# Swapping two DMA queues, a second weight set one part earlier, and another pacing of staged rows in a fused long-convolution and mixture-of-experts kernel

## Chip, cores and metric

The kernel runs on one core of a Trainium2 chip. The metric is the time of one execution in device microseconds (us); lower is better. Engines are named as in the profile: PE (matrix engine; PEld its weight loads), DVE (vector), ACT (scalar), POOL (GpSimd) and SP (which here only issues DMAs). A "q" behind an engine's name, as in ACTq, means its instruction queue.

## What is computed

```python
def _attn_ref(x, h):                      # x: (8, 5696, 128), h: (5696, 128), float32
    L = 2 * S
    Yf = np.fft.rfft(x, n=L, axis=1) * np.fft.rfft(h, n=L, axis=0)[None]
    return np.fft.irfft(Yf, n=L, axis=1)[:, :S, :]

def _moe_ref(x, w_gate, w1, w2):          # x: (45568, 128), 8 experts, hidden width 1024
    logits = x @ w_gate
    expert_idx = np.argmax(logits, axis=1)
    ...                                   # probs = softmax(logits), gate_w = probs of the chosen expert
    for e in range(E):
        mask = expert_idx == e
        out[mask] = gate_w[mask, None] * (np.maximum(x[mask] @ w1[e], 0.0) @ w2[e])
    return out
```

The output of the convolution is the token list of the second part: 8 x 5696 = 45568 tokens, each of which goes through one of 8 experts.

## The kernel before

The 8 batches are worked in three groups of 2, 3 and 3 (g0, g1, g2). A group goes through three stages. Stage a (`steps_a`) transforms 48 slices of a batch and stores them to DRAM (`U`). Stage b (`phase_b`) goes over 120 frequency items: it loads `uq` from `U`, makes `xp` on PE, multiplies by the filter on DVE, adds on POOL (`combine`; for the first `ALONE` = 20 items of g2 on DVE), transforms back (`vp`), copies on ACT (`save`, tile `vt`) and stores to `V`. Stage c (`phase_c`) makes token rows from `V`, finds each row's expert, and scatters the rows with indirect DMAs from POOL into `SR`, where rows are sorted by expert; `sort_one` issues one such scatter, and the rows still to be scattered stand in the list `sorts`. Stage a of the next group runs inside stage c of this one (`Guest`). In the text a1 is stage a of g1, b2 stage b of g2, and so on.

Beside this run the experts (`pipeline`): tiles of 256 sorted rows. One tile is loaded (`load`, tile `xr`, 7 buffers), transposed (`turn`, PE tile `mx`), and goes through four steps, each with six matmuls of `layer1` and six of `layer2`; in between, `relu` on ACT and DVE makes `hs`. `drain` copies the result on ACT (`ot`), `turn` transposes it back, `emit` scales it into `xr`, and two indirect DMAs from POOL (`deliver`) scatter the 256 rows to `out`. The four weight pieces of an expert (512 KB each) are loaded by `load_w`, under a condition that skips the load where the expert stays the same.

Tiles become available in parts: a part closes when a given slice of a group is sorted (`HALVES`), and `tables` then works out on DVE, in row vectors of one partition, which rows and which expert each of its tiles has. With the constants of before the parts have 37, 39, 28 and 81 tiles (182 of the 185 run always). The first three have one set of weight buffers, loaded from ACT's queue; the last has two, used in turn, loaded from SP's queue (`sets`, `home`).

While a stage c runs, POOL is taken by the sort, so finished expert tiles are not scattered but stored to DRAM (`leave`, array `STG`); the flag `state["defer"]` says so. Afterwards `recall` loads them back (tile `xb`), one every `BACK` = 6 steps of the pipeline, and their scatters join the same list `pending` as the fresh ones.

The order of instructions on each engine's queue is fixed when the program is made: `run` interleaves the streams by planned costs in units of `STEP`. One expert step costs one `STEP`, one item of stage b `MIX_B[g]`, one step of stage c `MIX_C[g]` (half of that after the last slice), and `HEAD` and `LEAD` are pauses of 8 and 6 steps at the start of stages b and c of g1 and g2. `SETTLE` is the planned pause of 8000 ns between the last sort scatter of a part and its first load. These costs set only the order; in the chip each engine takes its queue in order and waits for what it needs.

Of the kernel before, what the change touches and what calls it, by code (L numbers as in the profile page):

```python
# [29 lines left out]
RW = 130  # L30
# [40 lines left out]
def conv_moe(ctx: ExitStack, tc: tile.TileContext, I, out, B, S, D, E, F, split):  # L71
# [146 lines left out]

    rest_of = [nc.vector]
# [39 lines left out]
    def steps_a(gr, tag, bufs):  # L259
# [28 lines left out]
        def flush():  # L288
            while late:
                nc.sync.dma_start(*late.pop(0))  # L290
# [10 lines left out]
        def store(m):  # L301
# [7 lines left out]
            cp(uts[c][:, :, b * D : (b + 1) * D], srcv)  # L309
# [106 lines left out]
    def phase_b(gr):  # L416
# [3 lines left out]
        def load_m(qb):  # L420
# [6 lines left out]
            else:  # L427
                mt = sb.tile([K2, QB, P], F32, tag="mt", name=f"mt{g}_{q}", bufs=MT)
# [20 lines left out]
        state, banks, late = {}, {}, []  # L449
# [53 lines left out]
        def product(n):  # L503
# [17 lines left out]
            state[n] = (zt, xs)  # L521

        def combine(n):
            zt, xs = state[n]
            eng = nc.vector if g > 1 and n < ALONE else nc.gpsimd
            eng.tensor_tensor(out=zt, in0=zt, in1=xs, op=ALU.add)  # L526

        def inverse(n):
# [3 lines left out]
            zt, _ = state.pop(n)  # L532
# [4 lines left out]
        def save(n):  # L537
# [4 lines left out]
            nc.scalar.copy(outs_[qb][:, k0, c * cw : (c + 1) * cw], banks.pop(n)[:K2, :cw])  # L542
# [21 lines left out]
        for n in range(N + BLAGS[3] + 2):  # L564
# [12 lines left out]
            while late:  # L577
                nc.sync.dma_start(*late.pop(0))
# [17 lines left out]
    state["alone"], state["prepped"], state["defer"], state["now"] = True, False, False, 0  # L596
# [43 lines left out]
    def phase_c(gr, guest=None, after=None):  # L640
# [8 lines left out]
        state["defer"] = g > 0  # L649
# [64 lines left out]
        def turned(n, k):  # L714
# [3 lines left out]
            nc.scalar.copy(yts[n][:, k * cb : (k + 1) * cb, :], tv)  # L718
# [123 lines left out]
        for n in range(n_end + 1):  # L842
            for k in range(nsub):
# [56 lines left out]
        state["alone"] = state["defer"] = False  # L900

    def tables(pt, base):
# [56 lines left out]
        back = 2 if last else 1  # L959
# [40 lines left out]
    def sets(t):  # L1000
        return 2 if seq[t][0] is parts[-1] else 1
# [20 lines left out]
    def load_w(t, n):  # L1022
        pt, j = seq[t]
        z, fixed = home(t), j < sets(t)
        eng = nc.sync if pt is parts[-1] else nc.scalar
        if n == 0:
            ew = eng.value_load(pt.tab[0:1, 1, j : j + 1], min_val=0, max_val=(E - 1) * P)  # L1027
            ch = None if fixed else eng.value_load(pt.tab[0:1, 2, j : j + 1], min_val=0, max_val=1)  # L1028
# [7 lines left out]
        eng.dma_start(dst, WD[n, ds(ew, P), :], **kw)  # L1036
# [31 lines left out]
    def relu(t, k):  # L1068
# [7 lines left out]
        hss[t, k] = hs  # L1076

# [20 lines left out]
    leaving, staged, coming = [], [], []  # L1098
    slot = [0]

    def emit(t, count):
# [7 lines left out]
        else:  # L1109
            pending.extend([(xr, 0), (xr, 1)])  # L1110
# [230 lines left out]
```

## Time and profile before

| | us |
|---|---|
| median of 3 runs (2384.26 to 2411.04) | 2392.96 |
| the profiled execution's own time | 2398.87 |
| its span, first to last instruction | 2397.1 |
| PE / DVE / POOL / ACT busy | 2142.3 / 1583.0 / 1205.5 / 1096.4 |
| mean granted TensorE clock, share of full speed | 0.958 |

A busy time is the sum of the stretches in which an engine had an instruction running; a matmul that waits in the array counts as busy. The stages are read off by which lines run when: c0 with a1 to about 470 us, b1 to 770, c1 with a2 to 1050, b2 from 1094 to 1432, c2 to 1720; after that only experts run.

### The profile page before, as it was taken

Reading aid. Unit: us, or ns where it says so; the run is one execution under the profiler, and the core shown is the slowest. Engines: PE = TensorE matmul, PEld = TensorE weight load, DVE = VectorE, ACT = ScalarE, POOL = GpSimd, SP = SyncE. Lnnn points to the kernel's source line nnn. Section 1 sums busy time; section 2 is a strip of 40 time slices with the busy share of each in tenths; the row PEclk is TensorE's granted clock in tenths of the full one; section 3 lists DMA queues with packets and bytes.
Section 4 is the critical chain, followed back from the end, with each engine's and each line's share of the span. In section 5 each row is a group of like instructions: output and inputs, shape, how many; then the busy total and the mean of one; then the engine's idle time right before and its main releaser. Section 6 shows DMA issues by size and latency. Waiting matters only on the chain. (4 is left out here: it accounts for less than half of the span.)

```text
span 2397.1 us, 46980 instructions
## 1 busy us (share of the span) xinstructions
PE 2142.3 (89%) x14070; PEld 1765.9 (74%) x14070; DVE 1583.0 (66%) x3937; ACT 1096.4 (46%) x2389; POOL 1205.5 (50%) x1289
## 2 busy tenths in 40 slices
PE   7799688679999999978999999988788899999997
PEld 4666454346667787766677778887678889999997
DVE  3499645578988677867988875666644444555554
ACT  4577444323333566543334445555333344444443
POOL 5366437755545076672566651766634444333332
PEclk8899999889999999989999999999889999999999
DMA  9999999698987988867899886656344344333330
GB/s 268 285 298 309 272 293 265 187 262 230 241 234 216 248 234 236 256 165 202 221 245 242 236 224 161 168 153 179 95 145 126 121 135 138 112 115 114 111 114 29
DMA packets 245468, 472.46 MB, mean 197 GB/s; under 512 B 34385, under 2 KB 156295, under 8 KB 245216
## 3 DMA queue, kind: packets, MB, share of 16 engines
q1 hardware_dynamic: 207456, 372.03, 55.8%
q10 hardware_dynamic: 13824, 50.34, 6.8%
q0 software_dynamic: 23936, 47.09, 6.6%
q8 instruction: 114, 1.87, 0.3%
q14 instruction: 138, 1.13, 0.2%
HBM read 595.97 MB, written 171.92 MB: 320 GB/s over the span
## 5 line engine op out<-in xcount | busy, mean ns | idle before, releaser
L1073 DVE SCALAR_TENSOR_TENSOR hs<-mh,hs 128x512 fp32r<-128x512 f32 x728 | 502.0, 690 | 455.1 <-ACT hs L1071 371.0
L1065 PE MATMUL mh<-xtb,wb 128*128 128x256 f32 x4368 | 717.8, 300 | 64.0 <-DVE hs L1073 23.8
L1065 PEld LDWEIGHTS mh<-xtb,wb 128*128 128x128 f32 x4368 | 600.5, 193 | 142.5 <-issue 51.4
L1085 PE MATMUL ma<-hs,wb 128*128 128x256 f32 x4368 | 664.7, 289 | 7.8 <-DMA wb<-WD 6.8
L1071 ACT ACTIVATE hs<-mh 128x512 fp32r<-128x512 f32 x728 | 435.7, 599 | 511.0 <-PE mh L1065 348.3
L1085 PEld LDWEIGHTS ma<-hs,wb 128*128 128x128 f32 x4368 | 582.1, 193 | 10.3 <-DMA wb<-WD 8.1
L610 POOL DMA_INDIRECT SR<-rt,pi x384 | 407.7, 1062 | 311.4 <-issue 135.7
L1129 POOL DMA_INDIRECT out<-xr x276 | 270.2, 979 | 554.6 <-DVE xr L1103 500.8
L526 POOL TENSOR_TENSOR zt<-zt,xs 128x384 f32<-128x384 f32 (+1 forms) x340 | 308.5, 912 | 179.5 <-DVE xs L518 112.2
L542 ACT COPY vt<-vp 96x384 f32<-96x384 f32 (+1 forms) x360 | 158.6, 440 | 426.1 <-PE vp L534 331.8
L486 PE MATMUL xp<-uq,mt 96*128 96x384 f32 (+1 forms) x720 | 273.0, 461 | 33.6 <-DMA uq<-U 14.5
L534 PE MATMUL vp<-zt,mi 128*96 128x384 f32 (+1 forms) x720 | 273.9, 462 | 8.2 <-DVE xs L518 2.3
L511 DVE TENSOR_TENSOR zt<-xp,hh 128x384 f32<-128x384 f32 (+1 forms) x360 | 183.4, 509 | 69.3 <-PE xp L486 45.7
L534 PEld LDWEIGHTS vp<-zt,mi 128*96 128x96 f32 x720 | 106.7, 163 | 125.8 <-issue 78.2
L297 PE MATMUL pa<-xc,fcr 120*120 120x512 f32 x576 | 172.4, 432 | 22.4 <-ACT ut L309 10.4
L518 DVE SCALAR_TENSOR_TENSOR xs<-xp,hh 64x384 f32<-64x384 f32 (+1 forms) x360 | 185.5, 515 | 6.8
L516 DVE TENSOR_TENSOR xs<-xp,hh 64x384 f32<-64x384 f32 (+1 forms) x360 | 182.3, 507 | 6.9
L486 PEld LDWEIGHTS xp<-uq,mt 96*128 96x128 f32 x720 | 117.9, 195 | 62.6 <-issue 32.9
L297 PEld LDWEIGHTS pa<-xc,fcr 120*120 120x120 f32 x576 | 102.2, 193 | 60.8 <-ACT ut L309 10.8
L675 DVE TENSOR_TENSOR vr<-vq,vr 120x768 fp32r<-120x768 f32 x96 | 91.8, 958 | 68.9 <-ACT vr L674 46.1
L309 DVE COPY ut<-pa 120x512 f32<-120x512 f32 x96 | 65.6, 686 | 91.9 <-PE pa L297 60.5
L687 PE MATMUL yp<-vr,gcr 120*120 120x384 f32 x576 | 118.1, 340 | 5.7 <-ACT vr L674 2.5
(123 smaller groups left out, 2212.8 us busy)
## 6 DMA issues: line engine op xcount, KB each, us to landing
wb<-WD ACTq DMA_DIRECT2D x416, 512.0 KB
wb<-WD SPq DMA_DIRECT2D x312, 512.0 KB
vq<-V SPq DMA_DIRECT2D x64, 720.0 KB
U<-ut SPq DMA_DIRECT2D x48, 720.0 KB
uq<-U SPq DMA_DIRECT2D x60, 576.0 KB
V<-vt SPq DMA_DIRECT2D x60, 576.0 KB
xr<-SR SPq DMA_DIRECT2D x182, 130.0 KB
xt<-x SPq DMA_DIRECT2D x96, 240.0 KB
```

What stands on the lines that cost most here:

```text
L297: nc.tensor.matmul(banks[m][:QN, :], lhs, rhs, start=(k == 0), stop=(k == len(ops) - 1))
L486: nc.tensor.matmul(xp[:, :cw], mt[:, k0, :], uc, start=True, stop=True)
L511: nc.vector.tensor_tensor(out=zt, in0=x3, in1=hv[:, 0].broadcast_to([P, cb, D]), op=ALU.mult)
L518: nc.vector.scalar_tensor_tensor(out=xs[to], in0=x3[at], scalar=-1.0, in1=him, op0=ALU.mult, op1=ALU.mult)
L526: eng.tensor_tensor(out=zt, in0=zt, in1=xs, op=ALU.add)
L534: nc.tensor.matmul(vp[:K2, :cw], mi[:, k0, :], zt.rearrange("p b d -> p (b d)"), start=True, stop=True)
L610: s = nc.gpsimd.indirect_dma_start(out=SR[:, :], out_offset=IndirectOffsetOnAxis(ap=pi[:, b : b + 1], axis=0), in_=rt[:, b, :], in_offset= ...
L1065: nc.tensor.matmul(hp[:, u, :], wb[:, a, f, :], xt[:, b, :], start=(n == 0), stop=(n == 2))
L1071: done = nc.scalar.activation(hs[:, 0], hp, AF.Relu)
L1073: nc.vector.scalar_tensor_tensor(out=hs[:, 1], in0=hp, scalar=0.0, in1=hs[:, 0].bitcast(F32), op0=ALU.max, op1=ALU.subtract)
L1085: nc.tensor.matmul(accs[t], wb[:, a, f, :], hs[:, b, u, :], start=(k == 0 and u == 0 and n == 0), stop=(k == NPAIR - 1 and u == 1 and n == 2),
L1129: sc = nc.gpsimd.indirect_dma_start(out=out[:, :], out_offset=IndirectOffsetOnAxis(ap=xr[:, s, D + 1 : D + 2].bitcast(I32), axis=0), in_=x ...
```

## The change

- `HALVES`: the second part closes at slice 12 of 24 in place of 14, so that parts have 37, 33, 34 and 81 tiles.
- `PAIRED`: the third part has two weight sets as well. The second set takes buffers of the tag `mt` in place of `ld`, once stage a of g2 is done (`state["spare"]`); the `mt` tiles of b2 take buffers of `xt`, and `xb` tiles take two of `us`.
- All weight loads go to SP's queue. The stores to `U`, `V`, the filter array `HS` and `STG` go to ACT's queue.
- What is left of `sorts` after a stage c is no longer scattered ahead of the next stage b, but one scatter after each `save` of it. In stage c of g0 there is one more `sort_one` a step, and the two extra ones after the last slice are gone. `tables` is finished and `defer` cleared before the next stage b.
- A returned tile waits 4 steps after its load, the next is recalled only when both scatters of the last are out, and returned scatters have a list of their own: one goes out when no fresh one has for two steps, then none for three.
- Planner's costs: b1 0.6 to 0.55, c2 1.8 to 2.2 (`MIX_A` 0.6 to 0.45 is used only if slices of a1 are left over after c0).

```diff
-HALVES = ((16,), (14, 24), (24,))
+HALVES = ((16,), (12, 24), (24,))
-MIX_A = (0.0, 0.6, 0.8)
-MIX_B = (0.0, 0.6, 0.85)
-MIX_C = (1.0, 1.2, 1.8)
+MIX_A = (0.0, 0.45, 0.8)
+MIX_B = (0.0, 0.55, 0.85)
+MIX_C = (1.0, 1.2, 2.2)
-BACK = 6
+PAIRED = 2
...
         def flush():
             while late:
-                nc.sync.dma_start(*late.pop(0))
+                nc.scalar.dma_start(*late.pop(0))
...
-                mt = sb.tile([K2, QB, P], F32, tag="mt", name=f"mt{g}_{q}", bufs=MT)
+                mt = sb.tile([K2, QB, P], F32, tag="xt" if g > 1 else "mt", name=f"mt{g}_{q}", bufs=5 if g > 1 else MT)
...
-            nc.scalar.copy(outs_[qb][:, k0, c * cw : (c + 1) * cw], banks.pop(n)[:K2, :cw])
+            done = nc.scalar.copy(outs_[qb][:, k0, c * cw : (c + 1) * cw], banks.pop(n)[:K2, :cw])
+            if state["late"]:
+                sort_one(done.ins)
...
             while late:
-                nc.sync.dma_start(*late.pop(0))
+                nc.scalar.dma_start(*late.pop(0))
...
-            nc.scalar.copy(yts[n][:, k * cb : (k + 1) * cb, :], tv)
+            done = nc.scalar.copy(yts[n][:, k * cb : (k + 1) * cb, :], tv)
+            if g == 0:
+                sort_one(done.ins)
...
-                if n >= nu:
-                    sort_one()
-                    sort_one()
...
         if guest:
             yield from guest.rest()
+            state["spare"] = g > 0
+        chore(99)
+        state["alone"] = state["defer"] = False
+        state["late"] = True
         if after:
-            yield next(after)
+            yield from after
         while sorts:
...
-        chore(99)
-        state["alone"] = state["defer"] = False
...
     def sets(t):
-        return 2 if seq[t][0] is parts[-1] else 1
+        return 2 if seq[t][0].s >= PAIRED else 1
...
-        eng = nc.sync if pt is parts[-1] else nc.scalar
-            tag, bufs = ("ld", LD) if z else ("wb", 4)
+            tag, bufs = ("mt", MT) if z else ("wb", 4)
-        eng.dma_start(dst, WD[n, ds(ew, P), :], **kw)
+        nc.sync.dma_start(dst, WD[n, ds(ew, P), :], **kw)
...
             _, dst, xr = leaving.pop(0)
-            nc.sync.dma_start(dst, xr)
+            nc.scalar.dma_start(dst, xr)
...
     def recall(count):
-        if coming and coming[0][0] <= count - BACK // 2:
+        if coming and coming[0][0] <= count - 4:
             xr = coming.pop(0)[1]
-            pending.extend([(xr, 0), (xr, 1)])
-        if staged and not coming and not state["defer"] and count % BACK == 0:
-            xr = sb.tile([P, 2, RW], F32, tag="xt", name=f"xb{count}", bufs=5)
+            returned.extend([(xr, 0), (xr, 1)])
+        if staged and not coming and not returned and not state["defer"]:
+            xr = sb.tile([P, 2, RW], F32, tag="us", name=f"xb{count}", bufs=2)
...
-    def deliver():
-        xr, s = pending.pop(0)
+    def deliver(after=None):
+        paced[0] += 1
+        if pending:
+            xr, s = pending.pop(0)
+            if s:
+                paced[0] = 0
+            after = None
+        elif returned and paced[0] > 1:
+            xr, s = returned.pop(0)
+            paced[0] = -1
+        else:
+            return
...
+        if after is not None:
+            tc.add_manual_dep(sc, after.name, SYNC, reason="scatters are spread over the stage")
...
             while nw[0] < min(t + 3, hi) and seq[nw[0]][0].tabled and state["prepped"]:
                 was, n = user[nw[0]], nw[1]
+                if home(nw[0]) and not state["spare"]:
+                    break
```

## Rows read from the trace of the kernel before

**Rows 1.** The page's parts 1 and 2: busy time of each engine, then tenths in 40 slices of 60 us for PE and for the DMA engines.

```profile
PE 2142.3 (89%) x14070; PEld 1765.9 (74%) x14070; DVE 1583.0 (66%) x3937; ACT 1096.4 (46%) x2389; POOL 1205.5 (50%) x1289
...
PE   7799688679999999978999999988788899999997
...
DMA  9999999698987988867899886656344344333330
```

**Rows 2.** Windows by stage, all lines: stretch and length, then busy us (instructions) of PE, PEld, DVE, ACT and POOL, granted clock, share of the DMA engines, GB/s.

```profile
483.00:515.00 32.00, 21.58 (x51) 10.17 (x51) 21.63 (x39) 4.55 (x10) 17.22 (x19) 0.78 1.02 270
515.00:770.00 255.00, 245.43 (x1249) 169.55 (x1248) 226.16 (x415) 92.74 (x202) 134.96 (x135) 0.99 0.89 236
770.00:1050.00 280.00, 261.57 (x1891) 221.88 (x1890) 204.00 (x691) 168.71 (x386) 154.01 (x165) 0.98 0.81 227
1050.00:1094.00 44.00, 27.67 (x171) 25.90 (x170) 21.22 (x95) 10.45 (x24) 27.88 (x34) 0.73 0.71 186
1094.00:1432.00 338.00, 325.47 (x1875) 247.51 (x1874) 295.06 (x546) 133.30 (x281) 188.27 (x188) 1.00 0.88 232
1432.00:1720.00 288.00, 260.23 (x2072) 231.81 (x2071) 179.77 (x662) 152.92 (x360) 161.36 (x176) 0.98 0.60 157
1720.00:1746.00 26.00, 13.72 (x64) 12.84 (x64) 13.77 (x48) 4.33 (x9) 14.65 (x18) 0.57 0.27 74
```

**Rows 3.** Windows of `layer1` alone (L1065; a tile has 24 such matmuls): stretch and length, PE busy (instructions), PEld busy (instructions), clock, DMA share, GB/s.

```profile
0.00:1720.00 1720.00, 368.40 (x2080) 292.90 (x2081) 0.96 0.83 230
...
1746.00:1880.00 134.00, 66.40 (x406) 57.15 (x407) 0.95 0.44 136
1880.00:2040.00 160.00, 82.22 (x542) 71.94 (x541) 0.99 0.42 131
2040.00:2286.00 246.00, 139.63 (x952) 124.55 (x951) 1.00 0.36 116
```

**Rows 4.** PE in the stretch 1746 to 1880 us: its waits for weight loads (us in total, times, longest), then the timeline behind one change of expert (start, length, what; in brackets the idle time ahead of it).

```profile
PE mh L1065 <- DMA wb<-WD: 12.8, 5, 3.6
...
1788.04 1.62 PE L1065 MATMUL mh<-xtb,wb 128*128 128x256 f32 x6 [2.87 <-DMA wb<-WD]
1789.45 1.48 PE L1085 MATMUL ma<-hs,wb 128*128 128x256 f32 x6
```

**Rows 5.** Timelines of POOL, then of PE, between 1954 and 1962 us: scatters of a fresh tile (`xr`) and of a returned one (`xb`), and the transposes `mx` that come once in each tile.

```profile
1957.10 0.97 POOL L1129 DMA_INDIRECT out<-xr  x1 [3.92 <-DVE xr L1103]
...
1959.66 0.97 POOL L1129 DMA_INDIRECT out<-xb  x1 [0.31 <-issue]
1960.94 0.97 POOL L1129 DMA_INDIRECT out<-xb  x1 [0.30 <-issue]
...
1954.64 0.38 PE L182 MATMUL mx<-ident,ot 128*128 128x128 f32 x2
...
1961.77 0.44 PE L182 MATMUL mx<-ident,ot 128*128 128x128 f32 x2 [0.79 <-ACT ot L1095]
```

**Rows 6.** The scatters of returned tiles and their loads, by tile (count; length in ns min/median/max; first and last start).

```profile
L1129 POOL DMA_INDIRECT out<-xb x88: 972/974/1250, 1112.0 to 2043.3; - x88
L1124 SPq DMA_DIRECT2D xb<-STG x44: 203/416/1343, 1090.4 to 2034.5; - x44
```

**Rows 7.** From timelines of SP and POOL, one load of a returned tile and the scatter that waited for it, and the last scatter of the kernel; from SP's waits, its wait at the end (us in total, times, longest).

```profile
2004.61 0.33 SPq L1124 DMA_DIRECT2D xb<-STG  x1
...
2009.85 0.97 POOL L1129 DMA_INDIRECT out<-xb  x1 [2.02 <-DMA xb<-STG]
...
2386.09 0.97 POOL L1129 DMA_INDIRECT out<-xr  x1 [0.30 <-issue]
...
SPq L1337 <- DMA out<-xr: 10.3, 2, 9.4
```

**Rows 8.** Timelines of PE, then of ACT, between c1 and b2.

```profile
1073.93 1.72 PE L1065 MATMUL mh<-xtb,wb 128*128 128x256 f32 x6 [7.38 <-DVE hs L1073]
...
1082.32 1.65 PE L1065 MATMUL mh<-xtb,wb 128*128 128x256 f32 x6 [3.81 <-DVE hs L1073]
...
1073.31 5.06 ACTq L1036 DMA_DIRECT2D wb<-WD  x2
1080.94 0.60 ACT L1071 ACTIVATE hs<-mh 128x512 fp32r<-128x512 f32 x1 [7.35 <-DMA xr<-SR]
```

**Rows 9.** ACT's waits between 480 and 1740 us that ended with a weight load (us in total, times, longest); then, by source line, the DMA instructions of the moved weight loads and `V` stores on the queue that they leave (ns min/median/max).

```profile
ACT vt L542 <- DMA wb<-WD: 40.5, 24, 3.9
...
ACT vr L674 <- DMA wb<-WD: 14.1, 13, 1.9
...
L1036 ACTq DMA_DIRECT2D wb<-WD x416: 88/90/2097, 479.9 to 1870.7; - x139
...
L578 SPq DMA_DIRECT2D V<-vt x90: 305/359/1364, 127.5 to 1429.9; - x90
```

**Rows 10.** The start of b1: timelines of PE, then of POOL.

```profile
483.02 4.62 PE L486 MATMUL xp<-uq,mt 96*128 96x384 f32 x8 [14.10 <-issue]
495.97 1.62 PE L486 MATMUL xp<-uq,mt 96*128 96x384 f32 x2 [8.33 <-DMA uq<-U]
...
488.13 1.00 POOL L610 DMA_INDIRECT SR<-rt,pi  x1 [0.30 <-issue]
489.51 3.91 POOL L526 TENSOR_TENSOR zt<-zt,xs 128x384 f32<-128x384 f32 x4
```

More of the change, by code (lines that the diff above doesn't have):

```diff
@@ L448, in phase_b @@
         cutting = F3[g]
-        state, banks, late = {}, {}, []
+        zts, banks, late = {}, {}, []
         def filt(qb, k0):
@@ L595, in conv_moe @@
     state["base"] = base0
-    state["alone"], state["prepped"], state["defer"], state["now"] = True, False, False, 0
+    state |= {"alone": True, "prepped": False, "defer": False, "late": False, "spare": False, "now": 0}
     sorts, row = [], [0]
@@ L648, in phase_c @@
         vqs, rts, yts, gates = {}, {}, {}, {}
-        state["defer"] = g > 0
+        state["defer"], state["late"] = g > 0, False
         nu = NB // NI
@@ L958, in tables @@
         nc.vector.memset(tab[:, 2, :], 1)
-        back = 2 if last else 1
+        back = 2 if g >= PAIRED else 1
         nc.vector.tensor_tensor(out=tab[:, 2, back:], in0=ej[:, back:], in1=ej[:, : NT - back], op=ALU.not_equal)
@@ L1076, in relu @@
         hss[t, k] = hs
+        return done.ins
     def layer2(t, k):
@@ L1097, in conv_moe @@
     STG = dram.tile([STAGED, P, 2, RW], F32, name="STG")
-    leaving, staged, coming = [], [], []
-    slot = [0]
+    leaving, staged, coming, returned = [], [], [], []
+    slot, paced = [0], [0]
     def emit(t, count):
@@ L1109, in emit @@
         else:
[L1110 removed]
+            pending.append((xr, 0))
+            pending.append((xr, 1))
     def leave(count):
@@ L1172, in pipeline @@
                 recall(len(hist))
-                if pending:
-                    deliver()
-                elif t >= hi and not (any(hist[-1 - LAG :]) or leaving or staged or coming):
+                deliver()
+                if t >= hi and not (any(hist[-1 - LAG :]) or pending or leaving or staged or coming or returned):
                     return
-                yield STEP if turned < nrow or any(hist[-1 - LAG :]) else None
+                busy = pending or leaving or staged or coming or returned or turned < nrow or any(hist[-1 - LAG :])
+                yield STEP if busy else None
                 continue
@@ L1189, in pipeline @@
             yield STEP
+            done = None
             if act:
-                relu(t, k)
+                done = relu(t, k)
                 step = (t, k + 1) if k < NPAIR - 1 else (t + 1, 0)
@@ L1201, in pipeline @@
                 emit(to, len(hist))
-            if pending:
-                deliver()
+            deliver(done)
     def experts():
@@ L1213, in rest @@
     def rest():
-        work = None
         for gr in groups:
-            if work:
-                yield from work
-            guest, work = None, None
-            if gr.g + 1 < len(groups):
-                guest, work = Guest(groups[gr.g + 1]), phase_b(groups[gr.g + 1])
-            yield from phase_c(gr, guest, work)
+            more = gr.g + 1 < len(groups)
+            guest, after = (Guest(groups[gr.g + 1]), phase_b(groups[gr.g + 1])) if more else (None, None)
+            yield from phase_c(gr, guest, after)
     DONE = object()
```

15 lines of the change are left out of this document (8 added, 7 removed).

## The prediction

> **What bounds the kernel now.** I read the page's totals and slices first. PE is busy 89% of the span, no other engine over 66% [rows 1], so a gain must come from stretches where PE idles or runs slowly. The slices show three dips behind the dense start: about 480, 1050 and 1720 us, each where a stage c ends. The DMA engines are nearly full up to 1430 us and about a third busy at the end.
>
> The windows by stage put numbers on it [rows 2]. In b1 and b2 PE is busy 245 of 255 and 325 of 338 us. c1 leaves 18 us idle, c2 28. The two transitions hold more for their length: of 44 us before b2 PE is busy 28, at clock 0.73, and of 26 us after c2 14, at clock 0.57, near the lower level, 1.2 GHz.
>
> The windows of layer 1 give the experts' price [rows 3]. From 2040 us on a tile takes 246 / (952/24) = 6.2 us, with no idle time: the floor. Before it, 1746 to 1880 takes 7.9 us a tile and 1880 to 2040 takes 7.1. Those 294 us hold 39.5 tiles, 245 us of floor work, so 49 us are lost there, the largest block that this change touches. By 1720 us 2080/24 = 86.7 tiles are done, and 95 of the 182 remain.
>
> **The second weight set.** With one set, a new expert's pieces can be loaded only as the old ones fall free. PE waits 12.8 us for this in 1746 to 1880, and behind such a wait groups of six matmuls last 1.48 us, the pace of the lower clock [rows 4], where later ones last 0.88. Some four such groups behind each of four waits cost about 8 us more. The last part already has two sets, but its first loads also wait, some 3 us. The parts before it keep 104 tiles together, so about 17 two-set tiles are left behind c2. I take -22 us (bounds: -24, and 0 if the loads come late anyway). The price is eight more experts' loads of 2 MB in the third part, 16 MB: hidden in c2, whose DMA share is 0.60, and the tail at 0.44 [rows 2, 3]; were that room gone, they would cost 16 MB at 157 GB/s, about 100 us.
>
> **Returned scatters, paced.** The other half of the 49 us: where two fresh and two returned scatters follow one another on POOL, the next transposes come 0.79 us late and 7.1 us after the last, not 6.2 [rows 5]. 26 pairs at about 1 us make 26. The trace doesn't say why, nor show single ones. Two fresh scatters in a tile cost nothing after 2040 us, so a lone one may be free: -26 us. If each costs half a pair, 64 of them in the tail cost 32, or +6 us net. The nearest row is the free one; I take -16.
>
> **The same pacing leaves tiles over.** This I count in the planner's steps. Before, deferral lasts 6 + 48 x 1.2 + 5 x 0.6 + 8 = 75 steps in c1 and 6 + 48 x 1.8 + 5 x 0.9 = 97 in c2; at four steps a tile this makes 43 staged tiles, and the trace has 44 [rows 6]. One comes back every 6 steps: 18 in b2's 108, and 26 in 156 steps behind c2, which is 39 tiles, and so the last returned scatter is at 2043 us [rows 6]. The count holds.
>
> After, c1 defers 67 steps and c2 6 + 48 x 2.2 + 5 x 1.1 = 117: 46 staged. In a tile, fresh scatters take two steps, one step passes, one returned scatter goes. Its second half goes a tile later; the next load is recalled one step after that, needs four, and so just misses the next slot. That makes 12 steps, three tiles, for one staged tile. b2's 116 steps bring back 10, c2 starts with 7 over and ends with 36. The 95 tiles behind it are 380 steps: 32 come back, and about four are left after the last expert.
>
> There PE has nothing to cover them. A load takes 2004.61 to 2009.85, 5.2 us; two scatters 2 x (0.97 + 0.30) = 2.5; and the last scatter lands 9.4 us after it is made [rows 7]. With two buffers a buffer turns in about 17 us. Counted from the last fresh scatter (end 2387, landing at +9), the tile in progress lands at +11, the next at +13; the buffers then give +29, +31 and +46. So three left over cost 22 us, four 36, two 19, one 4. I take +30; bounds 0 (the count is wrong, or they slip in between) and +39.
>
> **Weights off ACT, stores onto it.** ACT waits for weight loads 40.5 us ahead of `vt` and 14.1 ahead of `vr` [rows 9], and in one place this reaches PE: ACT's two loads take 5.06 us, `relu` starts 7.35 late, and PE idles 3.81 [rows 8]. The 7.38 us wait beside it ends with DVE; the tables that keep DVE there stay. Of the 44 us before b2, 171 matmuls are worth 20 at the tail's pace (8.4 per us), so 24 are lost; I take -8 (bounds 0 and -15) for the load waits and the slow clock behind them. In the stages PE idles 10, 18, 13 and 28 us [rows 2]; a part of c1's and c2's is ACT's: -10 (bounds 0 and -28). c2 at 2.2 gets five more tiles to fill its gaps, about as many as b1 loses: -4. What comes onto ACT is 238 stores, which at SP's 0.36 us [rows 9] are 86 us of its queue; 416 loads at 0.09 us and their register work leave it. ACT is busy 46% [rows 1], so the difference is hidden. Behind a store that waits stand ACT's `vt` and `relu`, and PE waits for those.
>
> The Trainium skill, "DMA: Bandwidth & Descriptors", section "Issuing engines are not separate DMA queues", says that DMAs from the scalar, sync and GpSimd queues run on the same 16 engines, so starting them elsewhere saves only the issuer's time. By it these 22 us would be near 0, and the sum below +4 in place of -18: 2397 on the scale of the runs. No row here shows which of the two holds.
>
> **Drains spread over stage b.** Before, POOL's sort scatters of g0 run back to back until 489.2 us and only then come b1's adds; but PE then waits for `uq` until 496 in any case [rows 10]. So little is won. After, about 16 scatters go one to an item: POOL needs 1.0 + 0.3 for the scatter and 1.0 for the add, 2.3 us an item [rows 10]. PE has only about 1.2 us of work in one (an estimate: the eight `xp` matmuls of four items take 4.62 us at the low clock [rows 10], so 0.6 us an item at the high one, and as much for `vp`). By the planner's costs the first expert then starts some 36 items into b1, after the last scatter and `SETTLE`. PE idles 16 x 1.1 us, and about 0.6 in each of 15 more: 27 us, against 10 of the 32 before [rows 2]. Of the 17 I take 5 off, because b1 then has four tiles fewer where the DMA share is 0.89 [rows 2]: +12 (bounds 0 and +25). For g2 the first 20 adds are on DVE, and nothing is lost.
>
> **Sum.** -22 - 16 + 30 - 8 - 10 - 4 + 12 = -18 against the profiled execution's 2398.9, so 2381. The median of the runs is 6 us lower than that execution: 2375.
>
> **Rivals.** *No leftover* (the staged tiles do come back in time): the sum is -48, which gives 2345. For it speaks only that it needs a misread count; the count fits 44 and 2043 us.
>
> *SP's queue blocks stage b*, the one on the slower side: a weight load waits on SP until PE has left the old piece, and behind it stand `uq`, the matrices and filters of b1 and b2, called for five items (12 us) ahead. At a change of expert 2 MB go first, 8.9 us at 232 GB/s [rows 2]. From the point where a landing takes over 12 us PE waits; some ten changes fall in b1 and b2, and at half of 8.9 each this is +45, so 2420. Against it: SP already waited there for `V` stores. The same page of the Trainium skill ("Queues, rings and completion order") says that each DMA engine takes turns between queues but consumes one queue in order, which speaks for this rival; no run so far shows it.
>
> *The gains are nil* where PE only moves its waits: two sets give 0, pacing 0, and the leftover a little less: about 2395.
>
> **Chances.** Forecast 0.5 (own range 2355 to 2400), no leftover 0.2, SP blocks 0.17, nil 0.13. A measurement of this kernel tells about 1% from no change, that is 2369 and 2417. Forecast gives 0.2 faster and 0.3 same; with the others faster 0.4, same 0.43, slower 0.17. The range 2330 to 2420 takes in the first two rivals, with returned scatters free at its low end.
>
> **What would show it.** Right: no PE waits for `wb` between c2 and the end but at the start of the last part; 46 loads of `xb`; a tail after the last `layer2` in which only SP and POOL work, some 40 us long, not 13; the first `layer1` near 560 us. Wrong: `xp` waiting for `uq` through b1 and b2 (SP blocks), the last `out<-xb` before the last `out<-xr` (count), tiles over 6.5 us beside single returned scatters, or long waits of ACT ahead of `vt` for its own stores.

## Result and profile after

The changed kernel takes 2410.3 us in the median of 16 runs, the kernel before 2394.4 on the same chip: a ratio of 1.0068, 95% interval 1.0042 to 1.0093. It is 16 us slower, where I had forecast 18 us faster. The profiled execution has a span of 2406.5 us against 2397.1.

The page of the changed kernel, parts 1 and 2, the lines of [rows 1]:

```profile
PE 2130.5 (89%) x14070; PEld 1764.4 (73%) x14070; DVE 1581.5 (66%) x3937; ACT 1092.0 (45%) x2389; POOL 1207.1 (50%) x1289
...
PE   7788768867998899897989999998979999999995
...
DMA  9988979788888678866898886587656434344421
```

The totals are nearly the same; the shape is not. The tail is dense now. But the slices from the second to the fifth (60 to 300 us), where b0 runs, were 7, 9, 9, 6 and are 7, 8, 8, 7, and the DMA engines are no longer full there. Windows by stage, columns as in [rows 2]: first b0 in the kernel before, then, in the changed kernel, b0, b1 ahead of and behind the first expert's start, b2, c2:

```profile
118.00:280.00 162.00, 150.92 (x695) 102.98 (x693) 149.40 (x354) 113.91 (x246) 102.82 (x132) 0.98 1.00 302
```

```profile
119.00:307.00 188.00, 154.32 (x700) 107.47 (x700) 151.59 (x359) 115.31 (x249) 103.76 (x134) 0.98 0.89 265
504.00:586.00 82.00, 56.83 (x127) 24.56 (x128) 55.06 (x99) 13.75 (x29) 51.03 (x55) 0.81 0.90 240
586.00:789.00 203.00, 192.08 (x947) 134.28 (x946) 178.65 (x327) 70.74 (x155) 105.51 (x106) 0.96 0.83 228
...
1109.00:1446.00 337.00, 318.45 (x1792) 240.59 (x1791) 289.40 (x531) 129.85 (x269) 175.53 (x178) 0.98 0.83 226
1471.00:1765.00 294.00, 271.74 (x2234) 246.62 (x2232) 188.10 (x677) 159.17 (x378) 159.60 (x172) 1.00 0.67 189
```

b1's stretch without experts is 82 us, not 32 [rows 2]. From its first `yp` to its last `gb`, c2 takes 294 us (1471 to 1765), before 274 (1445 to 1719), for five tiles more. Layer 1 alone behind c2 (columns as in [rows 3]) shows the part that went as forecast:

```profile
1793.00:2373.00 580.00, 326.44 (x2214) 290.95 (x2214) 0.99 0.41 137
```

2214 matmuls are 92.25 tiles, so 6.29 us a tile, near the floor of 6.2; before, the same kind of stretch began with tiles of 7.9 and 7.1 us [rows 3]. What was lost lies ahead of it and at the end. The fresh tiles' scatters, the returned ones and their loads (as [rows 6]), and SP's loads and waits at the end (the line with x5 spans the last five loads; the two below it are the second and the third of these):

```profile
L1147 POOL DMA_INDIRECT out<-xr x272: 969/972/1006, 619.1 to 2379.3; - x136
L1147 POOL DMA_INDIRECT out<-xb x92: 969/971/1097, 1113.6 to 2393.9; - x92
L1132 SPq DMA_DIRECT2D xb<-STG x46: 238/337/1032, 1096.6 to 2389.7; - x46
...
2365.59 24.41 SPq L1132 DMA_DIRECT2D xb<-STG  x5
...
2368.07 0.34 SPq L1132 DMA_DIRECT2D xb<-STG  x1
...
2382.91 0.32 SPq L1132 DMA_DIRECT2D xb<-STG  x1
...
SPq L1132 <- DMA out<-xb: 19.9, 3, 14.4
```

46 tiles were staged, as counted. Nine returned scatters, those of four and a half tiles, come behind the last fresh one, the last of them 14.6 us later. PE's last layer ends at 2376, the kernel 30 us later; before, that gap was 14.

b0 was not in my sum at all. From first to last `xp` it takes 187 us (119.1 to 306.0), before 162:

```profile
L486 PE MATMUL xp<-uq,mt x240: 377/381/634, 117.9 to 279.9; 96*128 96x256 f32 x120
```

The timeline of the changed kernel in b0, PE, DVE and ACT:

```profile
202.15 0.42 DVE L514 TENSOR_TENSOR zt<-xp,hh 128x256 f32<-128x256 f32 x1
...
202.95 0.37 ACT L545 COPY vt<-vp 96x256 f32<-96x256 f32 x1 [0.51 <-PE vp L537]
203.01 0.31 ACTq L583 DMA_DIRECT2D HS<-hh  x1
...
203.34 0.58 ACT L470 COPY hh<-hp 64x512 f32<-64x512 f32 x1
...
203.59 0.67 PE L489 MATMUL xp<-uq,mt 96*128 96x256 f32 x2 [0.46 <-DVE xs L521]
...
204.30 0.42 DVE L514 TENSOR_TENSOR zt<-xp,hh 128x256 f32<-128x256 f32 x1 [0.85 <-PE xp L489]
```

An item takes three DVE instructions of 0.42 us, 1.27 of the 1.35 us that it lasted before, so DVE has almost no slack. Here it idles 0.85 us, because `xp` came late, and `xp` had waited 0.46 us for a product of DVE on an earlier item. `xp` waits so 30 times in 120 items, about every fourth.

### The profile page after: what moved, and what is told of

Read it like the earlier page. It is cut to its first block, busy times and chain, and to the rows that moved or that the text cites. A ratio compares the mean times of both kernels' runs of the same rounds, so it can differ in the third digit from the quotient of the medians.

```text
span 2406.5 us, 46954 instructions
## 1 busy us (share of the span) xinstructions
PE 2130.5 (89%) x14070; PEld 1764.4 (73%) x14070; DVE 1581.5 (66%) x3937; ACT 1092.0 (45%) x2389; POOL 1207.1 (50%) x1289
## 5 line engine op out<-in xcount | busy, mean ns | idle before, releaser
L1071 PE MATMUL mh<-xtb,wb 128*128 128x256 f32 x4368 | 697.5, 295 | 59.7 <-DMA wb<-WD 24.2
L1071 PEld LDWEIGHTS mh<-xtb,wb 128*128 128x128 f32 x4368 | 589.6, 191 | 128.4 <-issue 59.6
L1092 PE MATMUL ma<-hs,wb 128*128 128x256 f32 x4368 | 661.0, 288 | 11.8 <-DMA wb<-WD 11.7
L1092 PEld LDWEIGHTS ma<-hs,wb 128*128 128x128 f32 x4368 | 578.3, 192 | 14.4 <-DMA wb<-WD 14.3
L489 PE MATMUL xp<-uq,mt 96*128 96x384 f32 (+1 forms) x720 | 282.8, 476 | 45.3 <-DMA uq<-U 24.3
L537 PEld LDWEIGHTS vp<-zt,mi 128*96 128x96 f32 x720 | 112.1, 166 | 129.2 <-issue 78.4
L1147 POOL DMA_INDIRECT out<-xb x92 | 90.0, 978 | 124.3 <-ACT ot L1102 79.5
```

The lines of the kernel that those rows point to most:

```text
L489: nc.tensor.matmul(xp[:, :cw], mt[:, k0, :], uc, start=True, stop=True)
L537: nc.tensor.matmul(vp[:K2, :cw], mi[:, k0, :], zt.rearrange("p b d -> p (b d)"), start=True, stop=True)
L1071: nc.tensor.matmul(hp[:, u, :], wb[:, a, f, :], xt[:, b, :], start=(n == 0), stop=(n == 2))
L1092: nc.tensor.matmul(accs[t], wb[:, a, f, :], hs[:, b, u, :], start=(k == 0 and u == 0 and n == 0), stop=(k == NPAIR - 1 and u == 1 and n == 2),
L1147: sc = nc.gpsimd.indirect_dma_start(out=out[:, :], out_offset=IndirectOffsetOnAxis(ap=xr[:, s, D + 1 : D + 2].bitcast(I32), axis=0), in_=x ...
```

## Experiments

All results are ratios to the time of the kernel before on the same chip. Labels are in order of time; each group of runs that shares a chip is named by what the kernel before took there. (The groups at 2417 and 2398 carry the same chip number, so part of what is called a difference of chips may be one of time.)

| run | before, us | ratio | 95% interval |
|---|---|---|---|
| e1 b0's stores on SP | 2417 | 0.9972 | 0.9947 to 0.9997 |
| e2 sort before b | 2417 | 1.0062 | 1.0035 to 1.0088 |
| e3 recall sooner | 2417 | 1.0021 | 0.9992 to 1.0050 |
| e4 two sets for the last part alone | 2417 | 1.0132 | 1.0099 to 1.0166 |
| e5 old banks | 2314 | 1.0131 | 1.0107 to 1.0156 |
| e6 SP, late banks | 2314 | 1.0090 | 1.0065 to 1.0115 |
| e7 SP and recall | 2314 | 1.0019 | 0.9997 to 1.0040 |
| e8 queues as before | 2314 | 1.0166 | 1.0140 to 1.0192 |
| e9 changed kernel | 2419 | 1.0068 | 1.0044 to 1.0091 |
| e10 = e1 | 2419 | 0.9976 | 0.9952 to 0.9999 |
| e11 = e5 | 2419 | 1.0000 | 0.9971 to 1.0029 |
| e12 = e7 | 2419 | 0.9939 | 0.9914 to 0.9964 |
| e13 = e1 | 2398 | 0.9992 | 0.9969 to 1.0015 |
| e14 = e8 | 2398 | 1.0067 | 1.0046 to 1.0089 |
| e15 bursts | 2398 | 1.0136 | 1.0112 to 1.0160 |
| e16 shares as before | 2398 | 0.9849 | 0.9819 to 0.9880 |
| e17 c2's share as before | 2312 | 0.9959 | 0.9943 to 0.9976 |
| e18 all together | 2312 | 0.9891 | 0.9872 to 0.9911 |

Chips differ in the ratio too: e5 and e11 are one kernel, at 1.0131 and 1.0000. So sizes are taken only between runs of one chip, or between the chips at 2394 to 2419, where the changed kernel gave 1.0068 twice and e1's kernel 0.9972 to 0.9992. The second way holds for e2, e3 and e4, beside which the changed kernel was not run; that spread of 0.002 is 5 us.

**Stores of b0 (e1, e9, e10).**

```
             while late:
-                nc.scalar.dma_start(*late.pop(0))
+                (nc.sync if g == 0 else nc.scalar).dma_start(*late.pop(0))
```

> The changed kernel with one thing undone: in stage b of group 0 (b0) the stores of HS and V are issued by SyncE again, not by ScalarE; all else is as changed. Theory A, the stores slow b0: from the first inverse product of c0 back to the first forward product of b0, b0 takes 201 us after the change (119.1 to 319.6) and took 179 before (117.9 to 296.9), because each store issued by ScalarE (0.31 to 0.39 us) holds up the vt copy behind it, and the four PSUM banks come free later. Then b0 is back within 183 us and the time is about 20 us shorter, 2390. Rival B: b0 is longer for another reason (SyncE's queue, the order of the items): b0 stays at 195 to 201 us and the time stays within 5 us of 2410.

> The changed kernel itself, unaltered, as the measure for the three kernels run beside it on the same chip: the kernel before took 2394, 2417 and 2314 us on the chips so far, so that ratios taken on different chips can't be held against each other to half a per cent. Expected is the ratio first measured, 1.004 to 1.009.

> The changed kernel with the stores of HS and V in b0 on SyncE, once more, beside the changed kernel on the same chip. Theory, the stores on ScalarE lengthen b0 by 20 to 25 us: b0 (first to last xp) takes about 162 us against about 187 for the changed kernel, and the ratio is 0.008 to 0.011 lower than that of the changed kernel. Rival, the difference between 0.9972 and 1.0068 was one of chips: the two ratios agree within 0.004.

The first theory holds: 0.9976 against 1.0068 on one chip is 22 us. `xp` in b0 by tile, first e9, then e10 (count; ns min/median/max; first and last start; below it idle time ahead of it, by what ended it, of PE and its weight loads together: us, times):

```profile
L489 PE MATMUL xp<-uq,mt x240: 377/382/634, 116.9 to 303.5; 96*128 96x256 f32 x120
...
  DVE xs L521: 15.3, 30
```

```profile
L489 PE MATMUL xp<-uq,mt x240: 377/381/634, 115.0 to 274.3; 96*128 96x256 f32 x120
...
  ACT vt L545: 2.2, 2
```

186.6 us against 159.3, and the waits of `xp` for DVE's products, all of them PE's, are gone.

**Why a store costs so much (e5, e6, e11).** PE's and DVE's instructions stand in the same order in e1 and the changed kernel, but not their waits. Four PSUM banks serve `xp` and `vp`, and the planner's clock decides which one each gets. The first operation of the 120 `xp` of b0 waits, in the compiled programs, for:

```
                        ScalarE   VectorE   neither
before, and e1              108         8         4
changed                      55        44        21
e5, e11 (by hand)           114         1         5
e6 (by hand)                  0       118         2
```

In b1 and b2 these waits are the same in all of these programs but the kernel before. By the bank orders fixed in e5 and e6, a bank that ScalarE frees held the `vp` of the item six back, one that VectorE frees the `xp` of the item two back. e5 and e6 fix the banks by hand, `cx_tile(name, k)` giving bank k mod 4 in a0 and b0; only e6 has the stores on SP:

```
-xp = ps.tile([P, 512], F32, tag="cx", ..., bufs=4)
+xp = cx_tile(..., n)           # e6: n % 2
-vp = ps.tile([P, 512], F32, tag="cx", ..., bufs=4)
+vp = cx_tile(..., n + 2)       # e6: 2 + n % 2
```

> The changed kernel, stores of HS and V in b0 on ScalarE, with the four PSUM banks of xp and vp in a0 and b0 fixed by hand as the kernel before mostly had them: xp of item n takes the bank that the vt copy of item n - 6 frees (bank n mod 4), vp of item n the bank that the products of item n + 2 freed (bank n + 2 mod 4). In the compiled program of the changed kernel 55 of 120 xp wait for ScalarE and 44 for VectorE (before: 108 and 8); here 114 and 1. Engines, orders and work stay as changed. Theory A, bank choice: ScalarE's 0.31 to 0.39 us for each store cost nothing by themselves, they only moved the planned end of the vt copies, so that the planner hands xp the bank of the item two before, whose products end late: b0 takes about 162 us (first to last xp; 187 as changed) and the time is about 23 us shorter than that of the changed kernel, a ratio of 0.997. Rival B, the engine's time: the issues on ScalarE hold up the vt copies whatever the banks: b0 stays at 180 to 187 us, ratio 1.004 to 1.007.

> The mirror of the run with the old banks: stores of HS and V in b0 on SyncE as before the change, but banks of xp and vp fixed so that xp of item n takes the bank of xp of item n - 2 (freed by its products on VectorE) in all items, and vp that of vp two before. All else as changed. Theory A, bank choice: b0 takes 187 us or more (first to last xp) though ScalarE issues nothing, and the ratio is 1.005 to 1.015. Rival B, the engine's time: b0 takes about 162 us as with the stores on SyncE alone, ratio 0.997.

> The changed kernel, stores of b0 on ScalarE, the banks of xp and vp fixed as the kernel before mostly had them; once more, beside the changed kernel. On another chip b0 took 169.0 us in this form, 164.3 with SyncE's stores and the late banks, 159.9 with SyncE's stores and the planner's banks. Theory, the banks that the planner hands out make up most of b0's loss and ScalarE's issues the rest: b0 takes 167 to 172 us against 185 to 189 for the changed kernel. Rival, ScalarE's issues are all of it: 183 us or more.

`xp` in b0, e11 then e6:

```profile
L498 PE MATMUL xp<-uq,mt x240: 377/382/707, 117.1 to 283.9; 96*128 96x256 f32 x120
...
  ACT vt L554: 32.4, 39
```

```profile
L498 PE MATMUL xp<-uq,mt x240: 379/382/766, 115.4 to 279.7; 96*128 96x256 f32 x120
...
  DVE xs L530: 1.5, 6
```

Both pure theories fall. Stores on ScalarE with the old banks: 166.8 us (169.0 in e5), the waits now being for the `vt` copy (PE's own are 18 times, 13.9 us; the rest are its weight loads'). Stores on SP with the late banks: 164.3. Either alone costs 4 to 9 us against SP's stores with the planner's banks on the same chip (159.3 in e10, 159.9 in e7), both together 27. So the loss needs both: mending the banks alone takes 20 of the 27 us away, taking the issues off alone 22. In time, mending the banks gives 16 of the 22 us (1.0000 against 1.0068) and taking the issues off as well 6 more; for the other order there is no time on this chip. That the changed kernel mixes both kinds of bank, which e6 doesn't, may be part of it; that wasn't tried.

**Tiles left over (e3, e7, e12).**

```
-if staged and not coming and not returned and not state["defer"]:
+if staged and not coming and len(returned) < 2 and not state["defer"]:
```

> The changed kernel with one condition altered: the next staged tile is read back while one of the two scatters of the tile before it is still to be issued, not after both; the period of a staged tile goes from 12 steps of the expert pipeline (3 tiles) to about 8 (2 tiles). Theory A, staged tiles are left over behind the last expert and cost about 17 us at the end (TensorE ends at about 2376, the kernel at 2406.5; before 2384 and 2397): none is left over, the end lies 10 to 14 us behind the last matmul, and the time falls by 15 to 20 us to about 2392. Rival B: the pacing hides nothing, more scatters an expert tile slow the tail itself (506 matmuls in 60 us after the change): the tail gets slower by what the end gains, and the time stays within 5 us of 2410.

> The changed kernel with two things together: stores of b0 on SyncE, and the next staged tile read back while one of the two scatters of the tile before it is still to be issued. If the two effects add (0.9972 for the first, 1.0021 against 1.0068 for the second), the ratio is 0.991 to 0.993, some 20 us below the kernel before. If the second one's gain was only a matter of where b0 put the later stages, the ratio is that of the first alone, 0.997.

> The changed kernel with b0's stores on SyncE and staged tiles read back sooner, beside the same kernel without the sooner read. Theory, the left over staged tiles cost 11 to 17 us: the end lies 15 us behind the last matmul, not 30, and the ratio is 0.005 to 0.007 lower than with the stores alone. Rival, the sooner scatters slow the experts by as much as the end gains: the two ratios agree within 0.003.

e12 against e10 is 0.9939 to 0.9976, 9 us; e3 against the changed kernel 11. Both are less than was expected. Returned tiles in e12, and SP's wait at the end:

```profile
L1147 POOL DMA_INDIRECT out<-xb x92: 971/972/1461, 1109.5 to 2200.9; - x92
...
SPq L1355 <- DMA out<-xr: 14.2, 1, 14.2
```

The last returned scatter now starts at 2200.9, 200 us before the last fresh one; the end lies 16 us behind the last matmul, not 30. e7 missed both of its expected ratios on its chip; what the sooner recall gave there, only a run of e1's kernel on that chip could tell.

**The sort's last scatters (e2).** The loop over `sorts` stands ahead of `yield from after` again, and two `sort_one()` in each substep from `n >= nu`, as before the change; `state["late"]` stays off. The extra `sort_one` a step in the stage c of g0 stays.

> The changed kernel with one thing undone: the scatters of a sort that are left at the end of a stage c are issued there at once, as before the change, and the first turn of the next stage b is taken before them; the drains inside the copies of stage b are gone. Theory A, the spreading holds back the first experts: the first expert's transpose starts at 585 us after the change and at 516 before, though stage b1 starts only 21 us later; b1 fits 14.25 expert tiles until c1 starts, 18.75 before. Then the first expert starts 80 to 85 us nearer to b1's start, b1 fits 18 to 19 tiles again, and the time falls by 15 to 28 us, to 2382 to 2395. Rival B: the tiles lost in b1 are made up later, or the early gap of b1 is due to loads of U that come late on SyncE's queue (mean wait of the first forward products 3 to 11 us): the tiles come back in b1, yet the time stays within 6 us of 2410.

1.0062 is within the interval of the changed kernel, as rival B had it. Layer 1 and the returned tiles in e2:

```profile
L1074 PE MATMUL mh<-xtb,wb x4368: 276/281/822, 549.6 to 2390.4; 128*128 128x256 f32 x199
...
L1150 POOL DMA_INDIRECT out<-xb x98: 971/972/1095, 1143.5 to 2424.1; - x98
```

On the chip at 2419, the changed kernel's layer 1 runs from 591.8 to 2404.4. So the experts start 42 us sooner and end some 14 sooner. But 49 tiles are staged, and the end lies 44 us behind the last matmul, not 30. The gain ahead is there and is given back at the end.

**Two sets (e4).** `PAIRED = 3`.

> The changed kernel with one thing undone: only the last part of the tiles has two sets of expert weights, as before the change; the part ahead of it has one set again. My prediction put a gain of 22 us on the second set for that part. Theory A, the gain is there: the kernel is 15 to 25 us slower than the changed one, about 2430, with waits of TensorE for weights at every change of expert in the part ahead of the last. Theory B, the gain isn't there, because weights loaded by SyncE ahead of the need already come in time, or because SyncE's queue pays for the second set with waits: the time stays within 6 us of 2410.

1.0132 against 1.0068: the second set gives 15 us. Layer 1 and PE's weight waits behind c2 in e4:

```profile
1824.00:2430.00 606.00, 332.50 (x2236) 296.18 (x2236) 0.99 0.37 121
```

```profile
PE mh L1071 <- DMA wb<-WD: 10.6, 6, 2.9
```

2236 / 24 tiles in 606 us are 6.50 us each; e3 on that chip has 6.32 and no such wait.

**Queues outside b0 (e8, e13, e14).**

```
-nc.scalar.dma_start(*late.pop(0))           # U, V, HS; leave() likewise
+nc.sync.dma_start(*late.pop(0))
+eng = nc.sync if pt is parts[-1] else nc.scalar
-nc.sync.dma_start(dst, WD[n, ds(ew, P), :], **kw)
+eng.dma_start(dst, WD[n, ds(ew, P), :], **kw)
```

> The changed kernel with the exchange of queues undone everywhere: U, V, HS and staged tiles are stored by SyncE, weights of all parts but the last are issued by ScalarE; two sets for two parts, pacing and spread drains stay as changed. b0 then has its old banks, so the run stands beside the one with b0's stores alone on SyncE (0.9972). Theory A, my prediction: outside b0 the exchange is worth 22 us (8 between c1 and b2, 10 in the stages c, 4 by the mix of c2): 1.005 to 1.008. Theory B: outside b0 it is worth nothing, since SyncE's queue takes over the waits that ScalarE's had: 0.994 to 1.000.

> The changed kernel with b0's stores of HS and V on SyncE: the base for the three runs beside it, each of which alters one thing more. On two chips it stood at 0.9972 and 0.9976 of the kernel before; expected 0.995 to 1.000, unless the chip is like the one on which the kernel before took 2314 us.

> As the base, with the other queues as before the change too: U, V, HS and staged tiles stored by SyncE, weights of all parts but the last issued by ScalarE. Theory A, my prediction: the exchange outside b0 gives 22 us, so this run is 0.007 to 0.011 above the base. Rival B: it gives nothing, within 0.003 of the base.

e8 came out above both of its ranges, on the chip where e1's kernel was not run; e13 and e14 set the pair on one chip. e14 against e13: 0.0075, 18 us for the exchange outside b0. ACT's waits in c2 of e14 (1445 to 1763 us):

```profile
ACT hs L1078 <- DMA wb<-WD: 13.9, 7, 5.5
ACT vr L679 <- DMA wb<-WD: 11.5, 10, 1.9
```

c2, from first `yp` to last `gb`, takes 317 us in e14 and 301 in e13, where neither wait appears among the longest, and behind it a tile costs 6.44 us against 6.28, some 15 us in all. Between the start of c1 and that of b2, where I had put 8 us, the exchange gives 3. In b1 and b2 it costs. Layer 1 from b1's start to c1's and from b2's to c2's, e13 then e14:

```profile
477.00:787.70 310.70, 64.71 (x342) 48.19 (x342) 0.92 0.85 228
1090.60:1452.60 362.00, 129.39 (x684) 96.45 (x684) 0.98 0.83 226
```

```profile
479.30:783.70 304.40, 66.60 (x342) 49.31 (x342) 0.96 0.89 234
1089.60:1445.60 356.00, 130.34 (x684) 96.48 (x684) 0.98 0.85 226
```

The same tiles take 6 us more in each with the weights on SP, and in b1 PE waits 17.2 us for weights in e13 and 6.4 in e14.

**Pacing (e15).** `recall` every 6 steps, both halves put into `pending` after 3 steps, as before the change; the returned tiles keep two buffers of `us`, where the kernel before had five of `xt`.

> As the base, with the returned tiles read back and scattered as before the change: one read every 6 steps, its two scatters handed over together and issued in two steps in a row behind no wait for an activation. Theory A, my prediction: the pacing hides 16 us of waits on VectorE and on PSUM banks, which come back, while the 9 to 11 us of leftover tiles at the end go; the run is 0.002 to 0.004 above the base. Rival B: the bursts cost nothing once the tail waits for matmuls alone; with the leftover gone the run is 0.003 to 0.005 below the base.

e15 is 0.0144 above e13, 34 us, several times what theory A has. Behind c2, layer 1 in e13, then in e15 while its returned scatters run and behind the last of them, and PE's waits in e15:

```profile
1780.00:2360.00 580.00, 327.02 (x2217) 291.59 (x2216) 0.99 0.42 137
```

```profile
1790.00:2102.00 312.00, 157.05 (x1023) 137.35 (x1022) 0.98 0.48 157
2102.00:2408.00 306.00, 174.51 (x1188) 155.70 (x1188) 1.00 0.30 98
```

```profile
PE mh L1071 <- DVE hs L1079: 11.4, 5, 3.3
PE mx L182 <- ACT ot L1102: 7.7, 5, 2.0
```

6.28 us a tile become 7.3 while the returned scatters run and 6.2 behind them. The 58 scatters, 29 pairs, cost some 48 us over the floor of 6.2, 1.6 us a pair; against e13 the whole stretch loses some 40, though nothing is left over at the end. The waits are of the kinds of [rows 5]; all of those shown lie ahead of 2102. Whether it is the spacing or the wait for an activation that makes lone scatters cheap was not tried.

**Shares (e16, e17).**

```
-HALVES = ((16,), (12, 24), (24,))       # e16
+HALVES = ((16,), (14, 24), (24,))
-MIX_A = (0.0, 0.45, 0.8)                # e16
+MIX_A = (0.0, 0.6, 0.8)
-MIX_B = (0.0, 0.55, 0.85)               # e16
+MIX_B = (0.0, 0.6, 0.85)
-MIX_C = (1.0, 1.2, 2.2)                 # e16, e17
+MIX_C = (1.0, 1.2, 1.8)
```

> As the base, with the shares between the stages and the expert stream as before the change (0.6 for a1, 0.6 for b1, 1.8 for c2) and the first part of group 1 cut after 14 steps again, not 12. Theory A, the new shares cost what the sum leaves open: with fewer experts in b1 and c2 more is left for the tail, or c2 gets longer (303 us against 274 before) for no more than the tiles it takes in; undoing them gives 0.003 to 0.008 below the base. Rival B: a tile costs as much in a stage as in the tail, so that the shares only move work; within 0.002 of the base.

> The changed kernel with b0's stores of HS and V on SyncE and the share of stage c2 alone as before (1.8, not 2.2); a1, b1 and the cut after 12 steps stay as changed. Theory A, c2 is it: fewer tiles fall into c2, fewer are staged (46 so far, 41 with all shares undone), the end lies 16 us behind the last matmul, not 30; the ratio is 0.985 to 0.990. Theory B, a1, b1 and the cut are it: of the 34 us, 14 lay in b1 (285 against 271 us, for 1.6 tiles fewer besides) and 12 in b2 (337 against 325), which c2's share can't reach; the ratio is 0.992 to 0.997, lower than the base's 0.997 to 0.999 by the leftover tiles alone.

e16 against e13: 0.0143, 34 us, with the pacing the largest single part. Layer 1 from b1's start to c1's, e13 then e16, with PE's waits for weights there:

```profile
477.00:788.00 311.00, 64.71 (x342) 48.19 (x342) 0.92 0.85 228
...
PE mh L1071 <- DMA wb<-WD: 11.0, 4, 5.5
PE ma L1092 <- DMA wb<-WD: 6.2, 3, 4.6
```

```profile
476.00:779.00 303.00, 71.86 (x378) 53.68 (x378) 0.94 0.88 237
...
PE ma L1092 <- DMA wb<-WD: 7.2, 3, 6.7
PE mh L1071 <- DMA wb<-WD: 1.2, 1, 1.2
```

With the shares of before, b1 holds 1.5 tiles more in 8 us less: 8 + 1.5 x 6.3 = 17 us, of which 9 are weight waits. Another 6 lie between b2's start and c2's, and 14 at the end: 41 tiles are staged, not 46, and the end is 16 us behind the last matmul, not 30. c2 itself is even: with 2.2 it is 30 us longer for five tiles, which cost 31 in the tail. e17 shows the same split on another chip: 41 staged and 16 us at the end, while b1 takes 286 us and b2 332, as in e7 (282 and 335). So c2's share moves the end, and b1's loss belongs to the other three numbers; which of them wasn't tried. By the ratio e17 can't be judged, since e1's kernel wasn't run on that chip. Whether c2's share costs more than the end is open: e7, which has nothing left over either, stood 0.006 (14 us) above e17, on another chip with the same time before.

**All together (e18).** e16 with e3's recall and e2's order.

> The changed kernel with b0's stores on SyncE, the shares and the cut as before, staged tiles read back sooner, and a sort's last scatters issued before the next stage b as before; what stays of the change are the second weight set for two parts, weights on SyncE with the other stores on ScalarE, and returned scatters one at a time behind an activation. If the effects add, the ratio is 0.976 to 0.983: 0.985 for stores and shares, up to 0.006 for the earlier experts in b1 once nothing is left over at the end. If the sort's scatters before b1 only delay b1 by what the experts gain, 0.983 to 0.987.

0.9891, 25 us faster than the kernel before and clear of the noise, but short of both expected ranges, so the effects don't simply add. A size against e16 isn't known, as the chips differ; against e17, on the same chip, it is 16 us. Layer 1 behind c2, in all, then while returned scatters run and behind them, and the returned tiles:

```profile
1686.00:2266.00 580.00, 329.25 (x2233) 293.60 (x2232) 1.00 0.43 144
...
1686.00:2060.00 374.00, 211.59 (x1434) 188.84 (x1434) 1.00 0.50 168
2060.00:2266.00 206.00, 117.66 (x801) 104.75 (x799) 1.00 0.30 99
```

```profile
L1150 POOL DMA_INDIRECT out<-xb x88: 969/970/1156, 1076.1 to 2059.8; - x88
```

93 tiles at 6.23 us each, near the floor, and nothing left over.

## Why the prediction was wrong

It had the sign wrong: -18 forecast, +16 measured. Term by term, in us:

| step | forecast | measured | from |
|---|---|---|---|
| two sets | -22 | -15 | e4 |
| pacing, with its leftover | -16 + 30 | -34 | e15, e13 |
| of this the leftover | +30 | +9 to +14 | e3, e12, gap at the end |
| queues outside b0 | -18 | -18 | e14, e13 |
| drains | +12 | 0 in time | e2 |
| stores in b0 | 0 | +22 | e9, e10 |
| shares | -4 | +34, 14 of them leftover | e16, e13 |

**The step that failed first** is "ACT is busy 46% [rows 1], so the difference is hidden". The sentence behind it names the risk (behind a store stand ACT's copies, and PE waits for those), and I priced it at nothing. 46% is a mean over the whole span. In b0 ACT was busy 114 of 162 us before the change and 115 of 188 after, in a loop with DVE, PE and four banks, where `xp` and DVE have hardly any slack; there the stores cost 22 us. My windows [rows 2] begin at 483 us: b0 was not looked at, since no gain was claimed there. A row of the trace of before would have shown how tight the loop is. That the planner would hand out other banks, without which the stores cost 7 to 9 us of b0 and not 27, no such row shows.

**The second** is that I priced the shares as moves of tiles: "c2 at 2.2 gets five more tiles to fill its gaps, about as many as b1 loses". It is the larger miss, 38 us. c2's gaps were not filled (a tile costs there what it costs in the tail), b1 got longer as well as emptier (e13 against e16: 285 against 271 us from first to last `xp`, with 1.5 tiles fewer up to c1), and each tile more in c2 is a tile more to stage.

**Right in kind, off in size.** The leftover was there as counted, 46 staged and four and a half left over, but it cost 14 us and not 30: I let the buffers turn from the last fresh scatter on, while SP's 14.4 us wait for a buffer began at 2368.5, ahead of PE's end, and only 2.6 us of it lie behind the last fresh scatter. No wait for weights remains among PE's behind c2, and lone scatters are nearly free. The pacing gave more than its bound of -26, because a pair of returned scatters in a burst costs 1.6 us in e15, where I had put about 1 on each of 26. The first expert came at 590 us, where I had said near 560; 22 to 26 us of this are b0's, since it comes at 564 to 569 with b0's stores on SP (e1, e10, e13).

**Right by luck.** The queues outside b0 gave the 18 us forecast, but elsewhere: 3 us and not 8 between c1 and b2; 16 in c2 and 15 in the tail; and b1 and b2 lost 12, which I had at 0 unless SP blocked. The drains' 0 hides two effects as well: e2 gains 42 us at the first expert and ends with three tiles more staged.

**The rivals.** The Trainium skill, "DMA: Bandwidth & Descriptors", section "Issuing engines are not separate DMA queues", says that the starting engine saves only its own issue time. e14 agrees as far as it goes: what comes back are ACT's waits in its weight loads, 25 us in c2. But by it I had put the gain near 0, and it is worth 18. The rival *SP blocks* (the same page of the Trainium skill, section "Queues, rings and completion order") did not decide: `xp` waits for `uq` 24.3 us in all, six times, all in b1, where 11.7 were waited before, and e14, with the old queues, still waits 21.2. What SP's queue does cost is the 12 us in b1 and b2. *No leftover* and *the gains are nil* fall with the nine late scatters and with e4, e14 and e15.

**What stays open.** Without the leftover's own row the parts add to -11 us; the leftover is in two of them, pacing and shares, and taken once it makes -25. The whole is +16. A part of the gap can be seen in the tail, where the second set and the pacing do not add. Over a floor of 6.2 us a tile, the tail loses 51 us before (line below), 47 in e15, 28 in e4 and 8 in the changed kernel: undoing the pacing costs 39, undoing the second set 20, both 43.

```profile
1746.00:2380.00 634.00, 341.45 (x2256) 301.01 (x2257) 0.99 0.37 118
```

That leaves some 25 us. Each difference carries 8 to 10 us, six of them some 21, so this is little more than the noise. Why the ratios differ between chips was not found either.

## What to carry to other kernels

A mean busy share says nothing about a stage in which an engine is one link of a tight loop: read the engine in each stage that an edit touches, also where no gain is expected. After an edit, compare which operation each buffer waits for, not only the order of instructions: here the planner handed out buffers by its own clock, and a store of 0.3 us went with 0.85 us of idle time on DVE. An edit that gains in one place and leaves work for the end should be tried with the end mended, or its gain is not seen (e2). And a mean over a stretch should be split where its cause ends: the 6.7 us a tile behind c2 in e15 is 7.3 with bursts and 6.2 without.

## What was not expected of the hardware

A lone indirect scatter (0.97 us on POOL) behind an activation cost the matmuls at most 0.1 us a tile: 6.26 us while such scatters ran and 6.17 behind them (e18). In bursts a tile took 7.3 us (e15). And chips differ in more than scale: with the same program c0, from first `yp` to last `gb`, took 152 us in e7 and 171 in e12, with 281 and 251 GB/s moved meanwhile; the kernel before took 2312 to 2419 us in all, at a mean granted clock of 0.966 on the two faster chips and 0.958 to 0.959 on three of the slower ones. The cause is open.
